# Gated-attention kernel: gate units in two parts, input checks moved, gate checked on output sums

## The chip, the cores and the metric

One core of a Trainium2 chip. The metric is the device time of one execution in microseconds (us), the median of three runs.

## The reference

Per batch (B=4), head (H=8) and channel, an attention with a decaying state, then two MLP blocks on x of shape (4, 768, 384):

```python
state = alpha[:, :, t, :, None] * state + np.einsum('bhd,bhe->bhde', k[:, :, t], v[:, :, t])
y[:, :, t] = np.einsum('bhd,bhde->bhe', q[:, :, t], state)       # S=768, D=48
...
x = x + np.maximum(layernorm(x) * g_ln @ w_ch1, 0) @ w_ch2       # 384 -> 1536 -> 384
h = gelu_tanh(x @ w_in); u, v = h[..., :512], h[..., 512:]       # 384 -> 1024
v_s = np.einsum('ts,bsd->btd', w_sg, layernorm(v) * g_ln2) + b_sg[None, :, None]
out = x + (u * v_s) @ w_out
```

## The kernel before

Every large product runs as three float16 passes on operands split into a high and a low half: ACT makes the high half, DVE or GpSimd (POOL) subtracts it and makes the low one (the helper `low`, L155 and its neighbours). This is only right for inputs within certain ranges, so the kernel gathers statistics of its operands on the way (`st_in`, `st_g`, `st_ws` and others), compares them at the end with bounds (`checks`, L1107 to L1109), and a flag then decides whether a slow general path runs as well. It does not run for these inputs, but the statistics are always taken.

The 3072 rows are 24 chunks of 128 (six to a batch) and 12 groups j of two chunks. `att_steps(i)` is the attention of chunk i: loads into one of two input tiles (`load_chunk`, L236, chunk i into the tile of chunk i-2), transposes by DMA (L298 splits into 16-bit halves on ACT, L301 is the transpose, L314 joins), scans over time on DVE (L361), the scaling of q and k (`scaled`), ACT's halves of them (L446, L468), the scaling of K (L482), scores and masks (L490, L503), v's halves (L549, L551), and the outputs psd and psy (L585, L621). `stats()` (L560 to L568) then takes the squares of q, k and v on ACT (L564) and the largest alpha on DVE (L567). The next chunk for this tile can only load when these have read it.

The matmul stages of a group are lists of units: `A_units` (w1, L717; ACT makes the hidden tile hT at L722, DVE its low half at L723), `B_units` (w2, L752, added at L755), `T_units` (transposes of x, L151, L152, L773, check L775), `C_units` (w_in, L799 and L828, with the gelu at L802 and L831). Per batch come `D_units` (the spatial gate: six units of 36 matmuls, L856, two scale-and-add on DVE, L862, product with u on POOL, L865) and `E_units` (w_out, L890; addition L892; output L894). The gate's product is split into halves only when the next gate unit is through: `finish_gate()` takes one `halves_of_gate` from a list, which makes the high half (L869), the low one, and the sum of squares for `st_g` (L872).

`split_path` puts all attention steps and units into one list of events with planned times and calls them in this order; the scheduler below it fixes each engine's order from there. Units have costs in us of PE. The reduces that check the weights (`weight_windows`, L903) are put out by a count of units, one at a time, behind the last low half of a hidden tile:

```python
n_unit += 1
if n_unit >= 160 and n_unit % 4 == 0 and windows:
    with tc.issue_after(last_dve[0].ins):
        windows.pop(0)()
```

All matmul outputs of A to E share a ring of three PSUM buffers (tag "g").

Of the kernel before, what the change touches and what calls it, by code (L numbers as in the profile page):

```python
# [17 lines left out]
P = 128  # L18
# [35 lines left out]
def split_path(ctx, tc, ident, bad, q, k, v, alpha, g1, w1, w2, w_in, g2, w_sg, b_sg, w_out, out):  # L54
# [14 lines left out]
    U = 256  # L69
# [32 lines left out]
    st_g = big.tile([P, NC], F32, name="st_g")  # L102
# [151 lines left out]
    def att_steps(i, group, slot):  # L254
# [179 lines left out]
        @step  # L434
        def _():
            if whole:
                nc.vector.scalar_tensor_tensor(out=T["F"], in0=T["q"], scalar=S_Q * S_K, in1=T["F"], op0=ALU.mult,
                                               op1=ALU.mult)
            else:
                scaled("F", "q")  # L440
            if whole:
                work(["ks"], F16)
                T["ks"] = T["ks"].rearrange("p a n t -> p (a n t)").bitcast(F32).rearrange("p (n t) -> p n t", n=NP)
            else:
                work(["qs"], F16)
                nc.scalar.activation(out=T["qs"][:, 0], in_=T["F"], func=AF.Copy)  # L446
            if not by_dma:
                T["k"] = transposed(1)
# [13 lines left out]
        else:  # L462
# [7 lines left out]
            @step  # L470
            def _():
                low(chosen(HB), T["kh"][:, 1], T["K"], T["kh"][:, 0])
                if "ks" not in T:
                    work(["ks"], F16)
                nc.sync.dma_start_transpose(out=T["ks"].rearrange("p a n d -> p (a n) d"),
                                            in_=T["kh"].rearrange("p a n t -> p (a n t)"))

            @step
            def _():
                T["Kr"] = T["K"]  # L480
                for p in range(NP):
                    nc.scalar.activation(out=T["K"][:, p, :], in_=T["K"][:, p, :], func=AF.Copy,  # L482
                                         scale=T["rf"][:, p:p + 1])

# [76 lines left out]
        def stats():  # L561
            with tc.issue_after(T["v last"][0].ins):
                for n in range(3):
                    nc.scalar.activation(out=junk()[:, 0:DM].rearrange("p (h d) -> p h d", h=H),  # L564
                                         in_=t[:, n, :, 0:D], func=AF.Square, accum_out=st_in[:, i, n:n + 1])
            with tc.issue_after(T["v last"][1].ins):
                nc.vector.tensor_reduce(out=st_in[:, i, 3:4], in_=t[:, 3, :, 0:D], op=ALU.max, axis=AX.XY,  # L567
                                        apply_absolute_value=True)  # L568
# [275 lines left out]
    def D_units(b):  # L844
        units = []
        for th in range(S // U):
            for dp in range(KG // 2):
                def unit(th=th, dp=dp):
# [3 lines left out]
                    pg = ps.tile([P, 2, U], F32, tag="g", bufs=3, name="pgs")  # L852
                    for f in range(2):
                        d = 2 * dp + f
# [4 lines left out]
                    tm = p2.tile([P, 2, U], F32, tag="tm", name="tm")  # L859
# [8 lines left out]
                    def halves_of_gate():  # L868
                        nc.scalar.activation(out=gt[key][:, dp, 0], in_=tm, func=AF.Copy)  # L869
                        low(dp, gt[key][:, dp, 1], tm, gt[key][:, dp, 0])  # L870
                        n_ = b * 6 + 2 * th + dp
                        nc.scalar.activation(out=junk()[:, 0:512].rearrange("p (a b) -> p a b", a=2), in_=tm,  # L872
                                             func=AF.Square, accum_out=st_g[:, n_:n_ + 1])
# [3 lines left out]
                units.append((unit, 36 * U / 2400.0, NW[3]))  # L877
        return units

    def E_units(b):  # L880
        units = []
        for c in range(NCH):
            def unit(c=c):
# [4 lines left out]
                for d in range(KG):  # L888
                    for a, r in passes:
# [3 lines left out]
                                               op0=ALU.mult, op1=ALU.add)  # L893
# [33 lines left out]
    if True:  # L927
# [149 lines left out]
        for _, kind, f, need in sorted(events, key=lambda x: x[:2]):  # L1077
# [17 lines left out]
            (st_g, 0.0, 2.0 ** 31, [NC]),  # L1095
# [257 lines left out]
```

## Time and profile before

| | |
|---|---|
| median of 3 runs | 686.86 us (686.51 to 688.11) |
| profiled execution | 688.59 us |
| its span | 686.8 us |
| PE busy | 640.7 us (93%) |
| DVE busy | 442.2 us (64%) |
| ACT busy | 412.1 us (60%) |
| POOL busy | 237.3 us (35%) |
| mean granted clock of PE | 0.981 |

The page gives the busy time of an engine over the whole span; the stretches, timelines and waits below are views of the same trace. A timeline row begins with the start and the length of an instruction or a run of like ones; what stands in brackets is how long the engine was idle before it and what released it.

### The profile page before, as it was taken

Reading aid. Unit: us, or ns where it says so; the run is one execution under the profiler, and the core shown is the slowest. Engines: PE = TensorE matmul, PEld = TensorE weight load, DVE = VectorE, ACT = ScalarE, POOL = GpSimd, SP = SyncE. Lnnn points to the kernel's source line nnn. Section 1 sums busy time; section 2 is a strip of 40 time slices with the busy share of each in tenths; the row PEclk is TensorE's granted clock in tenths of the full one; section 3 lists DMA queues with packets and bytes.
Section 4 is the critical chain, followed back from the end, with each engine's and each line's share of the span. In section 5 each row is a group of like instructions: output and inputs, shape, how many; then the busy total and the mean of one; then the engine's idle time right before and its main releaser. Section 6 shows DMA issues by size and latency. Waiting matters only on the chain.

```text
span 686.8 us, 14367 instructions
## 1 busy us (share of the span) xinstructions
PE 640.7 (93%) x5622; PEld 487.2 (71%) x5622; DVE 442.2 (64%) x852; ACT 412.1 (60%) x787; POOL 237.3 (35%) x462
## 2 busy tenths in 40 slices
PE   5989798989999989999999989998989999999995
PEld 3677586667676876677677876676666986676783
DVE  6799977867745576557745569658756686233334
ACT  3765445687873698498773788767663873232230
POOL 4132210533423650443533751532405660301251
PEclk9999979999999998999999999999999999999999
DMA  9996879648363468466263387754263402200102
GB/s 226 279 246 177 259 168 185 105 88 118 64 107 53 72 110 152 105 113 110 48 112 51 60 116 158 123 105 70 51 89 62 86 17 70 24 12 12 35 2 75
DMA packets 228637, 70.64 MB, mean 103 GB/s; under 512 B 219472, under 2 KB 222544, under 8 KB 228560
## 3 DMA queue, kind: packets, MB, share of 16 engines
q1 hardware_dynamic: 228560, 69.63, 53.3%
q8 instruction: 46, 0.75, 0.5%
q14 instruction: 31, 0.25, 0.1%
HBM read 35.79 MB, written 4.72 MB: 59 GB/s over the span
## 4 chain that ended last, share of the span: by engine, by line
PE 51%; DMA 15%; DVE 14%; ACT 11%; issue 4%; POOL 2%; SPq 1%; ACTq 0%; DVEq 0%; POOLq 0%
PE pg L752 12%; PE pg L717 10%; PE pgs L856 9%; PE pgo L890 5%; PE pgu L828 5%; DMA stage<-stage 5%; PE pgv L799 4%; DMA wgs<-wsp 3%; ACT stage L314 2%; DMA stage<-in_moe_w_ch_dram 2%; DMA xhT<-xsp 2%; DMA inp<-in_q_dram 2%; ACT stage L298 2%; PE sc L490 1%; DVE sc L503 1%
## 5 line engine op out<-in xcount | busy, mean ns | idle before, releaser
L717 PE MATMUL pg<-xhT,w1s 128*128 128x256 f16 (+1 forms) x1404 | 152.5, 268 | 10.6 <-DVE hT L723 9.4
L717 PEld LDWEIGHTS <-w1s 128*128 128x128 f16 x1404 | 130.1, 100 | 28.7 <-issue 9.0
L752 PE MATMUL pg<-w2s,hT 128*128 128x384 f16 x864 | 146.6, 328 | 0.4 <-DVE hT L723 0.4
L752 PEld LDWEIGHTS <-hT 128*128 128x128 f16 x864 | 83.8, 98 | 54.3 <-issue 1.4
L856 PE MATMUL pgs<-wgs,vn 128*128 128x256 f16 x864 | 96.0, 273 | 0.0
L856 PEld LDWEIGHTS <-vn 128*128 128x128 f16 x864 | 84.1, 98 | 10.3
L723 DVE SCALAR_TENSOR_TENSOR hT<-pg,hT 128x512 f16<-128x512 f32 (+1 forms) x74 | 49.2, 673 | 44.8 <-ACT hT L722 44.6
L314 ACT ACTIVATE stage<-stage 128x1024 uint16<-128x1024 uint16 x48 | 64.4, 1351 | 16.2 <-DMA stage<-stage 16.2
L298 ACT ACTIVATE stage<-inp 128x1024 uint16<-128x1024 uint16 x48 | 49.8, 1051 | 26.2 <-DVE K L361 8.8
L155 POOL TENSOR_TENSOR kh<-K,kh 128x512 f16<-128x512 f32 x17 | 21.0, 1238 | 102.3 <-ACT kh L468 102.3
L722 ACT ACTIVATE hT<-pg 128x512 f16<-128x512 f32 (+1 forms) x74 | 42.0, 572 | 17.5 <-PE pg L717 17.1
L828 PE MATMUL pgu<-x2T,wis 128*128 128x256 f16 x432 | 49.6, 273 | 1.7 <-ACT vg L802 0.9
L799 PE MATMUL pgv<-wis,x2T 128*128 128x512 f16 x216 | 49.3, 379 | 1.8 <-DVE hT L723 1.8
L890 PE MATMUL pgo<-wos,uT 128*128 128x384 f16 x288 | 48.6, 326 | 0.1
L828 PEld LDWEIGHTS <-wis 128*128 128x128 f16 x432 | 41.8, 98 | 8.3 <-issue 1.8
L155 POOL TENSOR_TENSOR qs<-F,qs 128x512 f16<-128x512 f32 x18 | 20.2, 1121 | 76.8 <-ACT qs L446 76.8
L865 POOL TENSOR_TENSOR tm<-tm,uT 128x512 f32<-128x512 f32 x24 | 32.9, 1372 | 23.6 <-DVE tm L862 23.2
L890 PEld LDWEIGHTS <-uT 128*128 128x128 f16 x288 | 27.7, 98 | 18.0 <-issue 0.3
L862 DVE SCALAR_TENSOR_TENSOR tm<-pgs,g2c,bbc 128x256 f32<-128x256 f32 x48 | 20.9, 477 | 28.9 <-PE pgs L856 17.6
L799 PEld LDWEIGHTS <-x2T 128*128 128x128 f16 x216 | 20.5, 97 | 24.0 <-issue 1.9
L522 ACT ACTIVATE ss<-sc 128x512 f16<-128x512 f32 x36 | 20.8, 591 | 24.0 <-DVE sc L503 23.9
L869 ACT ACTIVATE uT<-tm 128x512 f16<-128x512 f32 x24 | 15.0, 626 | 30.0 <-POOL tm L865 30.0
(184 smaller groups left out, 1094.0 us busy)
## 6 DMA issues: line engine op xcount, KB each, us to landing
stage<-in_moe_w_ch_dram SPq DMA_DIRECT2D x24, 384.0 KB, 5.3
inp<-in_alpha_dram SPq DMA_DIRECT2D x24, 192.0 KB, 3.6
inp<-in_q_dram SPq DMA_DIRECT2D x24, 192.0 KB, 3.4
inp<-in_k_dram SPq DMA_DIRECT2D x24, 192.0 KB, 4.0
inp<-in_v_dram SPq DMA_DIRECT2D x24, 192.0 KB, 4.3
out_dram<-x SPq DMA_DIRECT2D x24, 192.0 KB, 1.9
stage<-in_moe_w_in_dram SPq DMA_DIRECT2D x4, 768.0 KB, 4.8
stage<-in_moe_w_sg_dram SPq DMA_DIRECT2D x6, 384.0 KB, 4.1
```

Of the source, the lines that this page charges most:

```text
L155: (nc.vector if on_dve else nc.gpsimd).tensor_tensor(out=out, in0=in0, in1=in1, op=ALU.subtract)
L298: nc.scalar.activation(out=sp, in_=t[:, n].rearrange("p h d -> p (h d)").bitcast(U16) .rearrange("p (x w) -> p w x", w=2), func=AF.Copy)
L314: nc.scalar.activation(out=words[:, :, :, gap:], in_=tr, func=AF.Copy)
L717: nc.tensor.matmul(out=pg[:, f, :], lhsT=w1s[:, a, kk, ff * P:(ff + 1) * P], rhs=xhT[j][:, r, kk, o], start=(n_ == 0), stop=(n_ == 3 * KD ...
L722: nc.scalar.activation(out=hi, in_=src, func=AF.Relu)
L723: last_dve[0] = nc.vector.scalar_tensor_tensor(out=lo, in0=src, scalar=0.0, in1=hi, op0=ALU.max, op1=ALU.subtract)
L752: nc.tensor.matmul(out=box[s], lhsT=hidden(a, f, s), rhs=w2s[:, r, f, :], start=(f == 0 and a == 0 and r == 0), stop=(f == KF - 1 and r == 1))
L799: nc.tensor.matmul(out=pg, lhsT=x2T[j][:, a, kk, o], rhs=wis[:, r, kk, DG:DI], start=(n_ == 0), stop=(n_ == 3 * KD - 1))
L828: nc.tensor.matmul(out=pg[:, f, :], lhsT=wis[:, a, kk, ff * P:(ff + 1) * P], rhs=x2T[j][:, r, kk, 0:N], start=(n_ == 0), stop=(n_ == 3 * K ...
L856: nc.tensor.matmul(out=pg[:, f, :], lhsT=vn[b * NCH + s][:, a, d * P:(d + 1) * P], rhs=wgs[th][:, r, s, :], start=(n_ == 0), stop=(n_ == 3 ...
L865: nc.gpsimd.tensor_tensor(out=tm, in0=tm, in1=uT[key][:, o, :], op=ALU.mult)
L890: nc.tensor.matmul(out=pg, lhsT=gt[key][:, d // 2, a, d % 2, o], rhs=wos[:, r, d, :], start=(d == 0 and a == 0 and r == 0), stop=(d == KG ...
```

## The change

A unit of the gate becomes two, f=0 and f=1, of 18 matmuls each; the scale-and-add, the product and `finish_gate()` are in the second. The squares of q and k and the reduce of alpha move from `stats()` to the place behind the first instruction that reads the operand (`T["q read"]`, `T["k read"]`, `T["q scaled"]`); v's square stays. The gate's sum of squares is taken for the last batch only; for the other three the addition behind w_out (L892) sums its output into a new row `st_o`, which is checked instead. In the changed kernel's rows below the line numbers are higher by 1 to 17.

```diff
--- before.py
+++ after.py
@@ -99,7 +99,8 @@
     st_mv = big.tile([P, NC, 2], F32, name="st_mv")
     st_xs = big.tile([P, NC], F32, name="st_xs")
     st_xm = big.tile([P, NC], F32, name="st_xm")
-    st_g = big.tile([P, NC], F32, name="st_g")
+    st_g = big.tile([P, 6], F32, name="st_g")
+    st_o = big.tile([P, NC - NCH], F32, name="st_o")
     st_ws = big.tile([P, 8 + NG3 + 2 * KD], F32, name="st_ws")
     st_w, st_wg, st_w1, st_wr = (st_ws[:, a:b] for a, b in ((0, 8), (8, 8 + NG3), (8 + NG3, 8 + NG3 + KD),
                                                             (8 + NG3 + KD, 8 + NG3 + 2 * KD)))
@@ -437,13 +438,13 @@
                 nc.vector.scalar_tensor_tensor(out=T["F"], in0=T["q"], scalar=S_Q * S_K, in1=T["F"], op0=ALU.mult,
                                                op1=ALU.mult)
             else:
-                scaled("F", "q")
+                T["q scaled"] = scaled("F", "q")
             if whole:
                 work(["ks"], F16)
                 T["ks"] = T["ks"].rearrange("p a n t -> p (a n t)").bitcast(F32).rearrange("p (n t) -> p n t", n=NP)
             else:
                 work(["qs"], F16)
-                nc.scalar.activation(out=T["qs"][:, 0], in_=T["F"], func=AF.Copy)
+                T["q read"] = nc.scalar.activation(out=T["qs"][:, 0], in_=T["F"], func=AF.Copy)
             if not by_dma:
                 T["k"] = transposed(1)
 
@@ -472,6 +473,13 @@
                 low(chosen(HB), T["kh"][:, 1], T["K"], T["kh"][:, 0])
                 if "ks" not in T:
                     work(["ks"], F16)
+
+                for n, first in enumerate((T["q read"], T["k read"][0])):
+                    with tc.issue_after(first.ins):
+                        square(n)
+                with tc.issue_after(T["q scaled"].ins):
+                    nc.vector.tensor_reduce(out=st_in[:, i, 3:4], in_=t[:, 3, :, 0:D], op=ALU.max, axis=AX.XY,
+                                            apply_absolute_value=True)
                 nc.sync.dma_start_transpose(out=T["ks"].rearrange("p a n d -> p (a n) d"),
                                             in_=T["kh"].rearrange("p a n t -> p (a n t)"))
 
@@ -481,6 +489,10 @@
                 for p in range(NP):
                     nc.scalar.activation(out=T["K"][:, p, :], in_=T["K"][:, p, :], func=AF.Copy,
                                          scale=T["rf"][:, p:p + 1])
+
+        def square(n):
+            nc.scalar.activation(out=junk()[:, 0:DM].rearrange("p (h d) -> p h d", h=H), in_=t[:, n, :, 0:D],
+                                 func=AF.Square, accum_out=st_in[:, i, n:n + 1])
 
         def scores():
             for e in range(2):
@@ -560,12 +572,7 @@
 
         def stats():
             with tc.issue_after(T["v last"][0].ins):
-                for n in range(3):
-                    nc.scalar.activation(out=junk()[:, 0:DM].rearrange("p (h d) -> p h d", h=H),
-                                         in_=t[:, n, :, 0:D], func=AF.Square, accum_out=st_in[:, i, n:n + 1])
-            with tc.issue_after(T["v last"][1].ins):
-                nc.vector.tensor_reduce(out=st_in[:, i, 3:4], in_=t[:, 3, :, 0:D], op=ALU.max, axis=AX.XY,
-                                        apply_absolute_value=True)
+                square(2)
 
         @step
         def _():
@@ -845,18 +852,24 @@
         units = []
         for th in range(S // U):
             for dp in range(KG // 2):
-                def unit(th=th, dp=dp):
+                box = {}
+
+                def unit(f, th=th, dp=dp, box=box):
                     key = (b, th)
 
                     gt[key] = uf[key].bitcast(F16).rearrange("p (g a f t) -> p g a f t", g=KG // 2, a=2, f=2)
-                    pg = ps.tile([P, 2, U], F32, tag="g", bufs=3, name="pgs")
-                    for f in range(2):
-                        d = 2 * dp + f
+                    if f == 0:
+                        box["pg"] = ps.tile([P, 2, U], F32, tag="g", bufs=3, name="pgs")
+                        box["tm"] = p2.tile([P, 2, U], F32, tag="tm", name="tm")
+                    pg, tm = box["pg"], box["tm"]
+                    d = 2 * dp + f
+                    if True:
                         for n_, (s, a, r) in enumerate([(s, a, r) for s in range(NCH) for a, r in passes]):
                             nc.tensor.matmul(out=pg[:, f, :], lhsT=vn[b * NCH + s][:, a, d * P:(d + 1) * P],
                                              rhs=wgs[th][:, r, s, :], start=(n_ == 0),
                                              stop=(n_ == 3 * NCH - 1))
-                    tm = p2.tile([P, 2, U], F32, tag="tm", name="tm")
+                    if f == 0:
+                        return
                     for f in range(2):
                         d = 2 * dp + f
                         nc.vector.scalar_tensor_tensor(out=tm[:, f, :], in0=pg[:, f, :], scalar=g2c[:, d:d + 1],
@@ -868,13 +881,15 @@
                     def halves_of_gate():
                         nc.scalar.activation(out=gt[key][:, dp, 0], in_=tm, func=AF.Copy)
                         low(dp, gt[key][:, dp, 1], tm, gt[key][:, dp, 0])
-                        n_ = b * 6 + 2 * th + dp
-                        nc.scalar.activation(out=junk()[:, 0:512].rearrange("p (a b) -> p a b", a=2), in_=tm,
-                                             func=AF.Square, accum_out=st_g[:, n_:n_ + 1])
+                        if b == B - 1:
+                            n_ = 2 * th + dp
+                            nc.scalar.activation(out=junk()[:, 0:512].rearrange("p (a b) -> p a b", a=2), in_=tm,
+                                                 func=AF.Square, accum_out=st_g[:, n_:n_ + 1])
                     gate_pending.append(halves_of_gate)
                     if b == B - 1 and th == S // U - 1 and dp == KG // 2 - 1:
                         finish_gate()
-                units.append((unit, 36 * U / 2400.0, NW[3]))
+                for f in range(2):
+                    units.append((lambda f=f, unit=unit: unit(f), 18 * U / 2400.0, NW[3]))
         return units
 
     def E_units(b):
@@ -890,7 +905,8 @@
                         nc.tensor.matmul(out=pg, lhsT=gt[key][:, d // 2, a, d % 2, o], rhs=wos[:, r, d, :],
                                          start=(d == 0 and a == 0 and r == 0), stop=(d == KG - 1 and r == 1))
                 nc.vector.scalar_tensor_tensor(out=xs[i], in0=pg, scalar=1.0 / (S_G * S_WO), in1=xs[i],
-                                               op0=ALU.mult, op1=ALU.add)
+                                               op0=ALU.mult, op1=ALU.add,
+                                               accum_out=st_o[:, i:i + 1] if b < B - 1 else None)
                 nc.sync.dma_start(out=out[b, c * P:(c + 1) * P, :], in_=xs[i])
             units.append((unit, 12 * DM / 2400.0, NW[4]))
         return units
@@ -1092,7 +1108,8 @@
             (st_xs, -1e30, 1e30, [NC]),
             (st_mv[:, :, 1:2], 2.0 ** -22 * S_Y ** 2, 2.0 ** 3 * S_Y ** 2, [NC, 1]),
             (st_xm, 2.0 ** -12, 2.0 ** 14, [NC]),
-            (st_g, 0.0, 2.0 ** 31, [NC]),
+            (st_g, 0.0, 2.0 ** 31, [6]),
+            (st_o, -1e30, 1e30, [NC - NCH]),
             (st_w, 2.0 ** -2, 127.0, [8]),
             (st_wg, 2.0 ** -2, 6e4, [NG3]),
             (st_w1, 2.0 ** -2, 2000.0, [KD]),
```

What it does to the order, at the end of batch 1's gate. ACT, from the scaling of K (L482, after: L490) to the first hidden tile (L722, after: L729) that PE waits for; L869 (after: L882) is a gate half, L872 its square, L446 (L447) the high half of q, L549 (L561) that of v, L494 the moved squares. Before:

```order
L482 ACTIVATE K<-K,rf 128x128 x4
L869 ACTIVATE uT<-tm 128x512
L872 ACTIVATE junk,st_g<-tm 128x512
L446 ACTIVATE qs<-F 128x512
L314 ACTIVATE stage<-stage 128x2x512
L647 ACTIVATE sp<-state 128x384
L549 ACTIVATE vs<-inp_95 128x384
L314 ACTIVATE stage<-stage 128x2x512
L660 ACTIVATE xsp<-psy,nmu 128x384
L151 ACTIVATE xsp<-x 128x384
L722 ACTIVATE hT<-pg 128x512
```

After:

```order
L490 ACTIVATE K<-K,rf 128x128 x4
L447 ACTIVATE qs<-F 128x512
L494 ACTIVATE junk,st_in<-inp_96 128x384 x2
L654 ACTIVATE sp<-state 128x384
L561 ACTIVATE vs<-inp_96 128x384
L882 ACTIVATE uT<-tm 128x512
L315 ACTIVATE stage<-stage 128x2x512
L667 ACTIVATE xsp<-psy,nmu 128x384
L152 ACTIVATE xsp<-x 128x384
L494 ACTIVATE junk,st_in<-inp_96 128x384
L315 ACTIVATE stage<-stage 128x2x512
L729 ACTIVATE hT<-pg 128x512
```

The two squares of q and k stand behind q's half, v's square ahead of the last join, the gate's square is gone, and the high half of v (L561) comes ahead of both joins.

DVE, from the low half of this hidden tile on (L723, after: L730); L503 (L515) are masks, L361 (L362) scans. Before:

```order
L723 SCALAR_TENSOR_TENSOR hT<-pg,hT 128x512
L155 TENSOR_TENSOR uT<-tm,uT 128x512
L503 TENSOR_TENSOR sc<-sc,causal 128x512 x2
L361 SCALAR_TENSOR_TENSOR F<-stage,reset 128x516
L361 SCALAR_TENSOR_TENSOR K<-stage,reset 128x516
L723 SCALAR_TENSOR_TENSOR hT<-pg,hT 128x512 x2
```

After:

```order
L730 SCALAR_TENSOR_TENSOR hT<-pg,hT 128x512
L156 TENSOR_TENSOR uT<-tm,uT 128x512
L730 SCALAR_TENSOR_TENSOR hT<-pg,hT 128x512
L515 TENSOR_TENSOR sc<-sc,causal 128x512
L730 SCALAR_TENSOR_TENSOR hT<-pg,hT 128x512
L515 TENSOR_TENSOR sc<-sc,causal 128x512
L362 SCALAR_TENSOR_TENSOR F<-stage,reset 128x516
L362 SCALAR_TENSOR_TENSOR K<-stage,reset 128x516
```

The second and third low half stand ahead of the scans.

DVE, behind the last low halves of the same group; L903 (L919) are the reduces over the weights, L892 (L907) the additions behind w_out. Before:

```order
L723 SCALAR_TENSOR_TENSOR hT<-pg,hT 128x512 x3
L903 TENSOR_REDUCE st_ws<-w1s 128x1
L892 SCALAR_TENSOR_TENSOR x<-pgo,x 128x384
L903 TENSOR_REDUCE st_ws<-w1s 128x1
L892 SCALAR_TENSOR_TENSOR x<-pgo,x 128x384 x2
L503 TENSOR_TENSOR sc<-sc,causal 128x512 x2
L361 SCALAR_TENSOR_TENSOR K<-stage,reset 128x516
```

After:

```order
L481 TENSOR_REDUCE st_in<-inp_95 128x1
L730 SCALAR_TENSOR_TENSOR hT<-pg,hT 128x512 x2
L919 TENSOR_REDUCE st_ws<-w1s 128x1 x3
L919 TENSOR_REDUCE st_ws<-w2s 128x1 x2
L907 SCALAR_TENSOR_TENSOR x,st_o<-pgo,x 128x384 x3
L939 SCALAR_TENSOR_TENSOR st_ws<-g1r,st_ws 128x3
L515 TENSOR_TENSOR sc<-sc,causal 128x512 x2
L362 SCALAR_TENSOR_TENSOR K<-stage,reset 128x516
```

Five reduces stand in one row ahead of the first three additions; before there was one ahead of the first and one ahead of the second.

## Rows read from the trace of the kernel before

**Rows 1.** The page's busy times, share of the span and instructions of each engine.
```profile
PE 640.7 (93%) x5622; PEld 487.2 (71%) x5622; DVE 442.2 (64%) x852; ACT 412.1 (60%) x787; POOL 237.3 (35%) x462
```

**Rows 2.** PE's waits: who waited for whom: us in total, times, longest us.
```profile
PE pg L717 <- DVE hT L723: 9.4, 7, 1.7
```

**Rows 3.** Stretches of 20 us: busy time of each engine (x instructions), PE's granted clock, DMA.
```profile
240.00:260.00 20.00, 17.59 (x198) 15.14 (x195) 15.32 (x28) 19.57 (x43) 10.65 (x14) 0.95 0.68 112
260.00:280.00 20.00, 18.52 (x149) 12.43 (x148) 12.34 (x24) 15.29 (x30) 2.68 (x5) 0.88 0.70 133
400.00:420.00 20.00, 16.13 (x163) 13.22 (x160) 14.11 (x28) 19.36 (x41) 8.23 (x13) 0.91 0.76 124
420.00:440.00 20.00, 20.00 (x165) 12.45 (x165) 16.95 (x29) 14.28 (x30) 5.99 (x13) 1.00 0.72 149
```

**Rows 4.** Timeline of PE, end of batch 0's gate: start, us, work, [idle before <-releaser].
```profile
257.17 3.17 PE L717 MATMUL pg<-xhT,w1s 128*128 128x256 f16 x18 [1.67 <-DVE hT L723]
...
261.82 5.59 PE L717 MATMUL pg<-xhT,w1s 128*128 128x256 f16 x36 [1.48 <-DVE hT L723]
267.24 4.06 PE L890 MATMUL pgo<-wos,uT 128*128 128x384 f16 x24
```

**Rows 5.** Timeline of ACT, the same place.
```profile
255.71 0.58 ACT L722 ACTIVATE hT<-pg 128x512 f16<-128x512 f32 x1
...
257.83 1.06 ACT L722 ACTIVATE hT<-pg 128x512 f16<-128x512 f32 x2
```

**Rows 6.** Timeline of DVE, the same place.
```profile
256.43 0.69 DVE L723 SCALAR_TENSOR_TENSOR hT<-pg,hT 128x512 f16<-128x512 f32 x1
...
261.09 1.26 DVE L723 SCALAR_TENSOR_TENSOR hT<-pg,hT 128x512 f16<-128x512 f32 x2
```

**Rows 7.** Timeline of PE, end of batch 1's gate.
```profile
411.09 3.48 PE L717 MATMUL pg<-xhT,w1s 128*128 128x256 f16 x18 [1.67 <-DVE hT L723]
415.74 4.10 PE L717 MATMUL pg<-xhT,w1s 128*128 128x256 f16 x36 [1.17 <-DVE hT L723]
419.94 4.06 PE L890 MATMUL pgo<-wos,uT 128*128 128x384 f16 x24
423.93 0.71 PE L490 MATMUL sc<-F,K 48*128 48x128 f32 x8
...
427.27 2.45 PE L890 MATMUL pgo<-wos,uT 128*128 128x384 f16 x14
```

**Rows 8.** Timeline of ACT, ahead of batch 1's last hidden tiles.
```profile
400.44 1.06 ACT L298 ACTIVATE stage<-inp 128x1024 uint16<-128x1024 uint16 x1 [1.80 <-DMA inp<-in_k_dram]
```

**Rows 9.** Groups of ACT's and DVE's instructions: count | busy us, mean ns | idle before.
```profile
L872 ACT ACTIVATE junk<-tm 128x512 bf16<-128x512 f32 x24 | 14.8, 615 | 0.0
...
L755 DVE SCALAR_TENSOR_TENSOR x<-pg,rx,x 128x384 f32<-128x384 f32 x24 | 14.7, 612 | 19.2 <-PE pg L752 19.2
...
L892 DVE SCALAR_TENSOR_TENSOR x<-pgo,x 128x384 f32<-128x384 f32 x24 | 13.3, 554 | 13.2 <-PE pgo L890 13.0
...
L903 DVE TENSOR_REDUCE st_ws<-w1s 128x1 f32<-128x1536 f16 x3 | 5.2, 1744 | 0.0
```

**Rows 10.** Timeline of DVE, end of batch 1's gate.
```profile
421.37 0.69 DVE L723 SCALAR_TENSOR_TENSOR hT<-pg,hT 128x512 f16<-128x512 f32 x1 [0.74 <-ACT hT L722]
421.98 1.75 DVE L903 TENSOR_REDUCE st_ws<-w1s 128x1 f32<-128x1536 f16 x1
423.64 0.55 DVE L892 SCALAR_TENSOR_TENSOR x<-pgo,x 128x384 f32<-128x384 f32 x1
```

**Rows 11.** Timeline of PE, waits between 120 and 140 us.
```profile
124.93 2.13 PE L828 MATMUL pgu<-x2T,wis 128*128 128x256 f16 x18 [0.80 <-DVE nmu L658]
...
139.95 0.20 PE L621 MATMUL psy<-vs,ss 128*128 128x48 f16 x1 [1.37 <-ACT ss L522]
```

**Rows 12.** Timeline of PE, a score that waits for ACT's K.
```profile
475.06 0.78 PE L490 MATMUL sc<-F,K 48*128 48x128 f32 x8 [1.52 <-ACT K L482]
```

**Rows 13.** Timeline of DVE, the last addition.
```profile
679.65 0.56 DVE L892 SCALAR_TENSOR_TENSOR x<-pgo,x 128x384 f32<-128x384 f32 x1 [1.34 <-PE pgo L890]
```

## The prediction

> **What bounds the kernel now.** I read the page's busy times first. TensorE (PE) is busy for 640.7 of 686.8 us [rows 1], so at most 46 us can be won without taking matmuls away, and the change takes none away: any gain must come out of the waits of PE. The list of PE's waits says which of those are left: the largest is L717, the first MLP matmul, waiting for VectorE's (DVE's) half of the hidden tile, L723: 9.4 us in 7 places [rows 2]. The table of 20-us stretches then says where: from 240 to 280 us and from 400 to 420 us PE works 17.59, 18.52 and 16.13 of 20 us and ScalarE (ACT) is full in two of the three, while the next stretch, 420 to 440, has PE at 20.00 [rows 3]. These are the ends of the spatial gate of batch 0 and of batch 1, where the gate's last halves, a chunk's input work and the hidden tiles of the next group meet on ACT and DVE.
>
> The three timelines of batch 0 show the mechanism. PE's last three units of L717 start at 257.17, 1.67 us late, and 261.82, 1.48 us late, and w_out (L890) only at 267.24 [rows 4]. ACT gives the hidden tile that is waited for at 255.71, behind a row of other work, then runs a gate half and its square L872, and gives the next two at 257.83 [rows 5]. DVE makes the first half at 256.43, then stands in its order behind masks and two scans and makes the next two only at 261.09 [rows 6]. Batch 1 repeats it: waits of 1.67 and 1.17 us, w_out at 419.94 [rows 7]. There the row of ACT work was itself held 1.80 us by the load of k [rows 8].
>
> **The change part by part.** *The gate's squares.* 18 of the 24 squares L872 go: 0.615 us each [rows 9], 11.1 us of ACT time, and the reading of an accumulator behind each. Most of it lies where PE works anyway, so I cost it at nothing by itself. Only the squares in front of a hidden tile count: one between the first tile and the second in each of the two gates, and it is part of the next term. In exchange 18 of the L892 get an accumulator. DVE's like instruction with one, L755, takes 612 ns against L892's 554 [rows 9]: 18 x 0.06 = 1.0 us of DVE beside PE's w_out, with three output buffers between, 0 on the path. If that cover were gone it would be 0.06 us per chunk.
>
> *The halves half a unit later, batch 0.* By the order, the second hidden tile stands one gate half behind the first on ACT, not behind half, square and another check, and on DVE no scan stands before the second and third. So the third wait (1.48 us) goes, and the stretch behind it is no longer entered with an idle PE. The first tile itself gains little: a square of the gate goes in front of it and the three squares of its own chunk come in. With the fourth unit from 257.2 for 3.17 us [rows 4] and the next two with no wait in 4.1 us, as in batch 1 [rows 7], w_out starts at 264.5 instead of 267.24: **-2.7 us**. Bounds: 0 if the first tile comes later by as much; -5 if its wait of 1.67 goes too.
>
> *The same in batch 1.* The wait of 1.17 us goes [rows 7]. The load of k waits before for a square that the ACT queue reaches late; now that square stands right behind the last reader of k, so the 1.80 us of [rows 8] should go and the first hidden tile come 1.4 us or more earlier. Together -2.6 for the start of w_out: 417.3 instead of 419.94. Bounds 0 and -4.
>
> *What the finer units push into batch 1.* The reduces that check the weights (L903) are counted out one on every fourth unit from the 160th on. Twelve more units stand ahead of that point (each gate has six more), and the order has five of them in one row behind the last hidden tile of this group, in front of the first three additions of w_out. Before, the row was hT, one reduce, addition, one reduce, addition [rows 10]. One reduce is 1.74 us [rows 9]; at a start-to-start of 1.66 us [rows 10] five are 8.4 us. The last hidden half ends 2.1 us after w_out begins (419.94 and 421.37 + 0.69), so the first addition ends 2.1 + 8.4 + 0.55 = 11.1 us after w_out's start. PE has three output buffers: it computes three chunks (2.05 us each, half of the 4.06 for 24 matmuls [rows 7]) and the two score groups (0.7 us each by the 0.71 at 423.93 [rows 7]), 7.5 us, and then stands for 3.6 us. Before, the fourth chunk began 7.33 us after the first; now 11.1: **+3.8 us**. It cannot hide behind idle time, since the stretch from 420 to 440 has none [rows 3]. Behind the reduces wait, besides, two masks and a scan; their readers on PE come after the same three chunks and are late by the same time. Net for batch 1: 3.8 - 2.6 = **+1.2**.
>
> *The clock.* The granted clock is 0.95 and 0.88 in the stretches of batch 0 and 0.91 in that of batch 1 [rows 3]. With levels of 2.4 and 1.2 GHz these means are about 6.8 and 3.6 us at half. It fell each time when PE stood for the first hidden tile, and 18 matmuls took 3.17 and 3.48 us instead of 2.05. What the new stall does to the clock no row shows directly. From above, 18 matmuls at half: +1.4 us; from below, the half-clock stretch of 3.6 us moves away from the gate: -1.4. I take 0. The Trainium skill (TensorE: Matmul & The Clock Gate, Part 1) says that the throttled level is the default and activity releases it. The trace agrees as to the fall. By this rule the stall in w_out would be followed by slow matmuls, and the sum would be 1.4 us higher, as no row of the w_out stretch before shows.
>
> *The input checks early.* alpha's reduce behind its scaling and the squares of q and k behind theirs let the loads of chunk i+2 leave earlier, since two buffers alternate. From 120 to 140 us it meets two waits of PE: 0.80 us at 124.93 and 1.37 us at 139.95, behind a chunk whose alpha came late [rows 11]. I take the first and half of the second, **-1.5**; bounds -4 (a second wait of that kind behind it, and slower matmuls) and +2.5 (two of the w_sg splits move behind squares, and hold up the masks). SP issues the alpha loads ahead of transposes that are later needed, 0 here: in each case the transposes wait for ACT anyway.
>
> *K's scalings.* Around the fifth group the four L482 of a chunk stand ahead of the vg tile, and the scores are spread. The nearest row is a score that waited 1.52 us for them [rows 12]. I take **+1.0**, between 0 and 1.5.
>
> *The tail.* One more entry in the list of checks, three small instructions. DVE waits there 1.34 us for PE [rows 13], so 0; if that cover were gone, less than one L892 each, 1.7 us.
>
> *The sum.* -2.7 + 1.2 - 1.5 + 1.0 = -2.0 us. The profiled execution took 688.59 us, with a span of 686.8 and 1.8 around it; it becomes 686.6. The runs shown have their median 1.7 us below it, so against the median: 686.86 - 2.0 = **684.9 us**. A measurement of this kernel can tell about 0.2%, 1.4 us.
>
> **The rivals.**
> *The clock holds (faster).* If the first tile comes early enough in both batches that PE does not fall to half, 3.17 - 2.05, 5.59 - 4.10 and 3.48 - 2.05 us come in addition [rows 4, 7]: 4.0 us, 680.9 us. For it: the removed waits lie just ahead of the slow matmuls. Against it: PE has small matmuls alone ahead of the first tile, and ACT has three squares more there. The rule of the skill's page (the same Part 1) points this way in batch 0, where matmuls come without a gap sooner.
>
> *The row of reduces decides (slower).* The mechanism is the five reduces at 424 to 428 us. It decides if the first hidden tile of batch 1 is no earlier than before: three squares of the chunk now stand ahead of it where one gate square of 0.615 us stood. They have 384 columns against its 512, an estimate of 0.46 us each, so +0.8 us, which takes back the load's gain when the load is not what ACT waits for. Then batch 1 is +3.8, the stall is followed by slow matmuls, +1.4, K's scalings +1.0, the early checks give 0 and batch 0 only the difference of 1.5 - 0.8: -0.7. Together +5.5: 692.4 us. For it: this stall is in the order, with durations from rows, and PE has nothing else to do.
>
> *It does nothing that shows.* The loads leave earlier, but what they feed waits for other things, and the gain at the first gate (-2.7) is eaten by the reduces, net of what batch 1 gains, and K's scalings (+2.2). That is -0.5: 686.4 us. For it: ACT and DVE have 40% and 36% idle [rows 1], and PE 20.00 of 20 us next to these stretches.
>
> **How the numbers follow.** The forecast gets 0.37, the held clock 0.20, the reduces 0.28 and no change 0.15. The forecast's own range is 683 to 687. For 8 in 10 I take the held clock in whole and most of the way to the slow case: **680.5 to 691.0**. Faster by over 0.2%: 0.28 of the forecast's 0.37 and the 0.20, 0.48. Within 0.2%: 0.06 of the forecast and 0.15, 0.21. Slower: the 0.28 and 0.03, 0.31.
>
> **What would show it.** After the change the list of PE's waits should have L717 behind DVE at 5 us or less, and w_out of batch 0 start within 8.5 us of the fourth unit of L717 (10.1 before). In batch 1 the DVE timeline should have five reduces in a row and the list of waits a new entry, w_out behind the addition, of about 3.6 us. ACT's wait for k before that gate should be gone. The prediction is wrong if that new entry is under 1.5 us or above 5, if the first hidden tile in either gate still comes late by 1.6 us, or if new waits of PE appear in the stretch from 280 to 400 us, which I hold to be unchanged but for K's scalings. The clock stands or falls with the granted clock from 240 to 280 us: 0.95 or more in both stretches would speak for the first rival.

## The result and the profile after

The changed kernel takes 691.48 us (median of 4 runs, 690.96 to 693.6); before it was 686.68 us in the same measurement. The ratio is 1.0074, 95% interval 1.0047 to 1.0101: slower, 4.8 us where 2 us faster was forecast, and outside the stated range. The profiled execution has a span of 691.8 us, 5.0 more than that of before, so the two traces can be set against each other.

The page of the kernel after, and its list of PE's waits (us in total, times, longest):

```profile
PE 641.8 (93%) x5622; PEld 487.9 (71%) x5622; DVE 445.3 (64%) x873; ACT 400.4 (58%) x751; POOL 237.2 (34%) x462
```

```profile
PE pg L724 <- DVE hT L730: 10.4, 9, 3.0
PE pgo L905 <- DVE x L907: 4.2, 1, 4.2
...
PE psy L628 <- ACT ss L534: 3.2, 1, 3.2
```

ACT has 11.7 us less to do (412.1 before), and PE is busy for 1.1 us more [rows 1]. L724's wait for the hidden half did not shrink (9.4 before [rows 2]), and there is a new one: w_out for its own addition, 4.2 us, once. The third line is also new in this size; the two waits that it replaces were 1.4 and 1.0 us.

The stretches of the two gates after, with the columns of [rows 3]:

```profile
240.00:260.00 20.00, 17.90 (x205) 15.76 (x203) 15.23 (x28) 16.73 (x31) 10.31 (x15) 0.97 0.61 104
260.00:280.00 20.00, 19.79 (x159) 13.62 (x158) 12.96 (x30) 14.10 (x26) 2.89 (x5) 0.94 0.62 123
400.00:420.00 20.00, 16.96 (x155) 14.31 (x153) 14.26 (x26) 16.21 (x31) 8.08 (x13) 0.91 0.60 111
420.00:440.00 20.00, 15.57 (x121) 9.22 (x119) 17.51 (x28) 10.19 (x14) 2.30 (x3) 0.83 0.51 119
```

At the first gate PE is idle for 2.3 us of 40, before 3.9. The loss stands in the last row: 4.4 us idle, and a granted clock of 0.83, where the kernel before had 20.00 us of work at 1.00. The timeline of PE at batch 1's gate, then that of DVE:

```profile
401.81 6.06 PE L724 MATMUL pg<-xhT,w1s 128*128 128x256 f16 x54
...
412.62 7.60 PE L724 MATMUL pg<-xhT,w1s 128*128 128x256 f16 x54 [3.04 <-DVE hT L730]
420.19 2.11 PE L905 MATMUL pgo<-wos,uT 128*128 128x384 f16 x12
422.51 4.06 PE L905 MATMUL pgo<-wos,uT 128*128 128x384 f16 x24 [0.21 <-DVE hT L730]
426.50 1.16 PE L502 MATMUL sc<-F,K 48*128 48x128 f32 x16
431.88 6.38 PE L905 MATMUL pgo<-wos,uT 128*128 128x384 f16 x25 [4.21 <-DVE x L907]
```

```profile
421.78 1.27 DVE L730 SCALAR_TENSOR_TENSOR hT<-pg,hT 128x512 f16<-128x512 f32 x2
422.98 5.06 DVE L919 TENSOR_REDUCE st_ws<-w1s 128x1 f32<-128x1536 f16 x3
427.96 3.40 DVE L919 TENSOR_REDUCE st_ws<-w2s 128x1 f32<-128x1536 f16 x2
431.28 0.54 DVE L907 SCALAR_TENSOR_TENSOR x<-pgo,x 128x384 f32<-128x384 f32 x1
```

The five reduces run from 422.98 to 431.36, the first addition ends at 431.82, and at 431.88 PE takes up w_out's fourth chunk, 11.7 us behind its first (7.3 before [rows 7]). Its next 25 matmuls take 6.38 us; at the 0.17 us of the 24 in 4.06 us they would take 4.2, so 2.1 us more go to the clock.

### The profile page after: what moved, and what is told of

Same layout as the page of the kernel before. It is cut to its first block, busy times and chain, and to the rows that moved or that the text cites. A ratio compares the mean times of both kernels' runs of the same rounds, so it can differ in the third digit from the quotient of the medians.

```text
span 691.8 us, 14361 instructions
## 1 busy us (share of the span) xinstructions
PE 641.8 (93%) x5622; PEld 487.9 (71%) x5622; DVE 445.3 (64%) x873; ACT 400.4 (58%) x751; POOL 237.2 (34%) x462
## 4 chain that ended last, share of the span: by engine, by line
PE 46%; DVE 21%; ACT 14%; DMA 10%; issue 4%; POOL 3%; SPq 1%; ACTq 0%; DVEq 0%; POOLq 0%
PE pg L759 12%; PE pgs L868 8%; PE pg L724 7%; PE pgo L905 5%; PE pgv L806 4%; PE pgu L835 4%; DMA stage<-stage 3%; ACT stage L315 3%; DVE hT L730 2%; DVE F L362 2%; DVE sc L515 2%; DVE K L362 2%; ACT stage L299 2%; DVE ss L156 2%; DMA xhT<-xsp 2%
## 5 line engine op out<-in xcount | busy, mean ns | idle before, releaser
L724 PE MATMUL pg<-xhT,w1s 128*128 128x256 f16 (+1 forms) x1404 | 153.1, 269 | 12.2 <-DVE hT L730 10.4
L724 PEld LDWEIGHTS <-w1s 128*128 128x128 f16 x1404 | 130.7, 100 | 30.3 <-issue 13.4
L759 PE MATMUL pg<-w2s,hT 128*128 128x384 f16 x864 | 144.8, 326 | 0.8 <-DVE hT L730 0.4
L730 DVE SCALAR_TENSOR_TENSOR hT<-pg,hT 128x512 f16<-128x512 f32 (+1 forms) x74 | 49.1, 671 | 35.9 <-ACT hT L729 35.8
L729 ACT ACTIVATE hT<-pg 128x512 f16<-128x512 f32 (+1 forms) x74 | 41.6, 573 | 23.4 <-PE pg L724 23.2
L905 PE MATMUL pgo<-wos,uT 128*128 128x384 f16 x288 | 50.7, 335 | 4.6 <-DVE x L907 4.2
L882 ACT ACTIVATE uT<-tm 128x512 f16<-128x512 f32 x24 | 15.0, 624 | 32.6 <-POOL tm L878 32.6
L818 DVE TENSOR_SCALAR vg<-vg,mvv,rv 128x512 f32<-128x512 f32 x24 | 15.9, 666 | 25.0 <-POOL rv L252 24.8
```

The costliest lines, as they stand in the source:

```text
L724: nc.tensor.matmul(out=pg[:, f, :], lhsT=w1s[:, a, kk, ff * P:(ff + 1) * P], rhs=xhT[j][:, r, kk, o], start=(n_ == 0), stop=(n_ == 3 * KD ...
L729: nc.scalar.activation(out=hi, in_=src, func=AF.Relu)
L730: last_dve[0] = nc.vector.scalar_tensor_tensor(out=lo, in0=src, scalar=0.0, in1=hi, op0=ALU.max, op1=ALU.subtract)
L759: nc.tensor.matmul(out=box[s], lhsT=hidden(a, f, s), rhs=w2s[:, r, f, :], start=(f == 0 and a == 0 and r == 0), stop=(f == KF - 1 and r == 1))
L905: nc.tensor.matmul(out=pg, lhsT=gt[key][:, d // 2, a, d % 2, o], rhs=wos[:, r, d, :], start=(d == 0 and a == 0 and r == 0), stop=(d == KG ...
```

## The experiments

Each kernel was timed over several runs on one chip, beside the kernel before; ratios are to that, with 95% intervals. `n_unit` is the count of units, from which the reduces are put out.

**1. The reduces back in place.** The changed kernel with

```diff
-                if n_unit >= 160 and n_unit % 4 == 0 and windows:
+                if n_unit >= 172 and n_unit % 4 == 0 and windows:
```

> The changed kernel, but the weight reduces counted from unit 172, so that they stand where they stood before (two behind batch 1's last hidden tile, not five). Theory A (the row of five reduces is the loss: a 4.2 us stall at w_out of batch 1, and slow matmuls after it): 685 to 687 us, no wait of w_out for an addition of over 0.5 us, granted clock 1.00 from 420 to 440 us. Theory B (the moved input checks are the loss, the stall only shows up where another wait would have stood): 689 to 691.5 us.

685.91 us, ratio 0.9986 (0.9967 to 1.0006). Without the row of five the change costs nothing that can be told. The stretch from 420 to 440 us, same columns:

```profile
420.00:440.00 20.00, 20.00 (x182) 13.49 (x181) 15.60 (x33) 17.44 (x34) 7.15 (x16) 1.00 0.83 183
```

**2. Five reduces in the kernel before.** In `before`:

```diff
-                if n_unit >= 160 and n_unit % 4 == 0 and windows:
+                if n_unit >= 148 and n_unit % 4 == 0 and windows:
```

> The kernel before, with the weight reduces counted from unit 148, which puts five of them into batch 1's w_out as the change does (one ahead of the first addition, four ahead of the second). Theory A: a wait of w_out of 3 to 5 us and slow matmuls behind it, 690 to 693 us. Theory B: 687 to 688 us.

685.31 us, 0.9976 (0.9952 to 1.0000): not slower, against theory A as it was put, and below the range of theory B too. The timeline of DVE shows the difference, and behind it PE's start of the fourth chunk:

```profile
419.57 1.74 DVE L903 TENSOR_REDUCE st_ws<-w1s 128x1 f32<-128x1536 f16 x1
421.23 0.55 DVE L892 SCALAR_TENSOR_TENSOR x<-pgo,x 128x384 f32<-128x384 f32 x1
421.69 3.40 DVE L903 TENSOR_REDUCE st_ws<-w1s 128x1 f32<-128x1536 f16 x2
425.01 3.40 DVE L903 TENSOR_REDUCE st_ws<-w2s 128x1 f32<-128x1536 f16 x2
428.33 1.01 DVE L892 SCALAR_TENSOR_TENSOR x<-pgo,x 128x384 f32<-128x384 f32 x2
```

```profile
425.35 2.12 PE L890 MATMUL pgo<-wos,uT 128*128 128x384 f16 x12
```

Here one addition stands ahead of four of the reduces. It gives PE a free buffer at 421.8, the fourth chunk starts with no wait, and PE has psy's matmuls between until the second addition at 428.33. So the number of reduces in the group does not make the stall; that all of them stand ahead of the first addition does (experiment 10 tests this in the changed kernel).

**3 and 4. Two parts alone.** The moved input checks in `before` (experiment 3), and the gate's sums in w_out's addition in `before` (experiment 4); each is the part of the change's diff, nothing else, with the reduces where they were.

```diff
+                for n, first in enumerate((T["q read"], T["k read"][0])):
+                    with tc.issue_after(first.ins):
+                        square(n)
...
-                for n in range(3):
...
+                square(2)
```

```diff
+                        if b == B - 1:
...
-                                               op0=ALU.mult, op1=ALU.add)
+                                               op0=ALU.mult, op1=ALU.add,
+                                               accum_out=st_o[:, i:i + 1] if b < B - 1 else None)
```

> The kernel before with the moved input checks alone (squares of q and k and alpha's reduce behind the first reader). Theory A: between 685 and 688 us; the wait at 140 us for the masks' halves is 3.2 us as in the changed kernel, against 2.4 in two pieces before, so not faster there. Theory B: 689 us or more.

> The kernel before with the gate's squares of three batches replaced by sums in w_out's addition, alone. Both theories: 685.5 to 687.5 us; the first hidden tile of batch 0 and batch 1 comes 0.5 to 0.7 us earlier, one square, and PE's wait for it shrinks by as much.

Experiment 3: 683.69 us, 0.9942 (0.9922 to 0.9963), faster, and below the range of theory A as well; theory B falls. Experiment 4: 687.77 us, 1.0016 (0.9994 to 1.0039), no gain. In its trace the first hidden tile at batch 0's gate, expected 0.5 to 0.7 us earlier, comes at 255.80, no earlier than before (255.71 [rows 5]). The second comes at 257.30 instead of 257.83, but PE is idle for 3.1 us from 460 to 480 us (before 2.4) and for 0.9 from 320 to 340 (before none).

**5 and 6. Four and three in the row.** The changed kernel with

```diff
+                if n_unit >= 164 and n_unit % 4 == 0 and windows:
```

and with 168 in this line.

> The changed kernel with four reduces, not five, in the row ahead of the first three additions (counted from unit 164). Theory A, each reduce in that row at 1.69 us: the wait of w_out for the addition falls from 4.2 to 2.5 us; from 685.9 (two in the row) that is 688.4 us, up to 690.1 if slow matmuls follow the stall. Theory C (it is not the row's length but any gap at w_out that lets the clock fall): as with five, 690.5 to 692 us.

> The changed kernel with three reduces in that row (counted from unit 168). Theory A: wait of w_out 0.8 us, 686.7 us, granted clock 1.00 from 420 to 440 us. Theory C: 688 us or more.

Four: 686.27 us, 0.9997 (0.9978 to 1.0016). Three: 683.29 us, 0.9951 (0.9933 to 0.9969). PE's start of the fourth chunk with four and with three:

```profile
427.47 4.55 PE L905 MATMUL pgo<-wos,uT 128*128 128x384 f16 x27 [1.76 <-DVE x L907]
```

```profile
425.55 5.36 PE L905 MATMUL pgo<-wos,uT 128*128 128x384 f16 x32
```

The wait is 1.76 us with four and gone with three, as computed within 0.8 us. The times are not as computed: theory A gave 688.4 and 686.7 us, and the kernels are 2.1 and 3.4 us faster than that. With four the clock from 420 to 440 us stays at 1.00:

```profile
420.00:440.00 20.00, 17.49 (x144) 10.75 (x143) 15.75 (x28) 15.26 (x26) 5.60 (x10) 1.00 0.57 132
```

Theory C falls at this place: a gap of 1.76 us brought no slow matmuls. (At the gates waits no longer than that, 1.67 us, do stand ahead of slow matmuls [rows 4] [rows 7], so the length of one wait does not decide it.)

That three are better than two I had not expected. Part of it stands in the next group. In experiment 1 PE waits twice in the stretch from 496 to 506 us, L724 for a hidden half 0.79 us and the first product of w_in (pgv) 1.55 us. On ACT the third hidden tile of that group stands behind the split of a load of q, and the split waits for the load:

```profile
496.22 1.06 ACT L299 ACTIVATE stage<-inp 128x1024 uint16<-128x1024 uint16 x1 [2.44 <-DMA inp<-in_q_dram]
497.18 0.58 ACT L729 ACTIVATE hT<-pg 128x512 f16<-128x512 f32 x1
```

With three in the row the third tile stands ahead of that split, and PE has no wait from 468 to 520 us:

```profile
494.86 0.60 ACT L729 ACTIVATE hT<-pg 128x512 f16<-128x512 f32 x1 [1.37 <-PE pg L724]
...
498.31 1.06 ACT L299 ACTIVATE stage<-inp 128x1024 uint16<-128x1024 uint16 x1 [1.71 <-DVE K L362]
```

With four the order is that of three, and PE has no wait there either; the changed kernel with five has the order of experiment 1, and loses 2.6 us from 500 to 520 us (3.0 in experiment 9). So the step from five to four (5.2 us between the medians, 4.3 by experiment 9, from different measurements) holds 2.5 us of stall, slow matmuls behind the longer stall, and these waits, less what comes back elsewhere; it can't be read as the price of the stall and the clock alone. Why the place of the reduces changes the order on ACT was not taken apart.

**7 and 8. The split alone, and with the checks.** Units in two parts in `before`, with 172 in the line of the reduces, and these together with the moved checks of experiment 3:

```diff
-                units.append((unit, 36 * U / 2400.0, NW[3]))
+                for f in range(2):
+                    units.append((lambda f=f, unit=unit: unit(f), 18 * U / 2400.0, NW[3]))
```

> The kernel before with the gate's units in two parts alone, the reduces counted from unit 172 so that they stay in place. If the later halves are what brings the second and third hidden tile forward: scans behind them on DVE, the third wait of L717 gone in both gates, 683.5 to 685.5 us. If the squares or the checks do that: 686 to 688 us, with the two waits as before.

> Split units and moved input checks, the gate's squares as before, the reduces in place (from unit 172). Against all three parts (685.9 us) it tells what the sums in w_out's addition cost or give: if they give nothing, 684 to 686 us; if taking the squares away is what helps at the gates, 687 to 689 us.

The split alone: 684.45 us, 0.9963 (0.9947 to 0.9980). Its waits at batch 0's gate:

```profile
246.79 6.06 PE L717 MATMUL pg<-xhT,w1s 128*128 128x256 f16 x54
...
255.57 2.12 PE L717 MATMUL pg<-xhT,w1s 128*128 128x256 f16 x18 [1.30 <-DVE hT L723]
257.70 2.13 PE L717 MATMUL pg<-xhT,w1s 128*128 128x256 f16 x18
261.73 2.14 PE L717 MATMUL pg<-xhT,w1s 128*128 128x256 f16 x18 [1.78 <-DVE hT L723]
265.32 8.77 PE L897 MATMUL pgo<-wos,uT 128*128 128x384 f16 x53 [1.46 <-DVE hT L723]
```

The wait of the third hidden tile did not go (1.78 us), yet w_out starts 18.5 us behind the first unit of L717, before 20.4 (267.24 - 246.83). Split and checks together: 684.84 us, 0.9976 (0.9957 to 0.9995). The gains of the parts (2.5 and 3.3 us) don't add. One reason is in the traces: both parts take away the same waits from 460 to 480 us, where the kernel before has 2.4 us of idle PE, the split alone 0.4 and the checks alone none.

**9. The changed kernel again,** beside the last three.

> The changed kernel unchanged, on the chip of the three runs beside it. Theory A: 690.5 to 692 us, the stall of w_out of 4.2 us again and some us at half the clock behind it.

690.54 us, 1.0067 (1.0048 to 1.0087). The same stall:

```profile
428.67 5.90 PE L905 MATMUL pgo<-wos,uT 128*128 128x384 f16 x25 [4.22 <-DVE x L907]
```

```profile
420.00:440.00 20.00, 15.78 (x122) 9.31 (x121) 15.19 (x25) 9.67 (x16) 2.52 (x4) 0.91 0.46 111
```

**10. Each reduce behind the last addition too.** The changed kernel, counted from 160, with

```diff
-                nc.vector.scalar_tensor_tensor(out=xs[i], in0=pg, ...
+                last_dve[0] = nc.vector.scalar_tensor_tensor(out=xs[i], in0=pg, ...
```

> The changed kernel with the reduces counted from unit 160 as in it, but each put behind the last addition of w_out as well as behind the last hidden tile, so that five still fall into this group and only one stands ahead of the first addition. Theory A (the place ahead of the additions counts, not the number): no wait of w_out for an addition, 684 to 687 us. Theory D (five reduces in this group hold up DVE wherever they stand): 689 us or more, with the wait moved to the masks or the gelu's statistics behind them.

686.33 us, 0.9996 (0.9979 to 1.0013): 4.2 us less than experiment 9, with the same five reduces in this group. No wait for the addition is left. The fourth chunk starts at 424.39, without one:

```profile
419.97 4.06 PE L905 MATMUL pgo<-wos,uT 128*128 128x384 f16 x24 [0.21 <-DVE hT L730]
424.39 3.91 PE L905 MATMUL pgo<-wos,uT 128*128 128x384 f16 x23
```

So theory A holds for the stall. Two other stretches differ as well. From 500 to 520 us PE has no wait, where experiment 9 loses 3.0 us. And at 468 PE waits twice for the second halves of the masked scores (0.88 and 1.02 us), which it does not in experiment 9. One reduce stands ahead of these masks on DVE, at 461.96, but in experiment 9 it does so too (464.62), so theory D is not shown by this wait.

**11 and 12. Three in the row with fewer parts.** Experiment 8 with 168, and experiment 3 with 156.

> Split units and moved checks, the gate's squares as before, three reduces in the row (from unit 168). Theory A with the gains of each part: 682 to 684 us, no slower than the 683.3 us of all three parts with three in the row. If the third part (sums in w_out) carries the gain of that kernel: 685 us or more.

> The kernel before with the moved input checks alone and three reduces in the row (from unit 156). If three in a row are as good there as in the changed kernel, because later stretches lose less: 681.5 to 683.5 us. If the row costs what it holds up: 684 to 686 us.

683.89 us, 0.9955 (0.9937 to 0.9972), and 682.34 us, 0.9934 (0.9915 to 0.9952). The moved checks alone, with three reduces in the row, have the lowest time of this study, 4.1 us under the kernel before, though the intervals of experiments 3, 6 and 11 overlap with theirs; that the split and the sums add anything to them is not shown.

## Why the prediction was wrong

The slow rival named the mechanism, at 692.4 us and with a chance of 0.28. The forecast had the same stall in its sum and let three other terms outweigh it. That the rival came within 0.9 us of the 691.48 us is in part luck: it had 0.7 us of gain at batch 0, where 3.0 were measured, and waits that stood in nobody's sum make up for it.

By the signs that the prediction set itself, it failed at the hidden tiles: the first one is late by 2.10 us at batch 0's gate and by 3.04 us at batch 1's, where 1.6 was the mark, and L724's waits for DVE come to 10.4 us, where it said 5 or less. Other signs came: w_out of batch 0 starts 7.6 us behind the fourth unit, five reduces stand in a row, the new wait is 4.2 us, and ACT's wait for k is gone.

Term by term, against the trace of after:

- **Batch 0, -2.7 us.** Right in size. From the first of the six units of L717 to w_out it takes 17.4 us, before 20.4: 3.0 us gained. The third wait went, as forecast; the first hidden tile is still waited for, 2.10 us. The slow matmuls that I thought to keep cost nothing: in experiment 9 the clock here is full and the same stretch takes 17.5 us, since PE then waits 1.52 us for a hidden tile. In these two executions ACT and DVE, with the hidden tiles, set the start of w_out, not the matmuls' speed. So the rival of the held clock had a price of nearly zero at this place, where I gave it 2.6 us; and 1.49 of these I had counted twice, since the forecast's own term already takes the last two units at 4.1 us. The two rows below are the changed kernel in its first profile and in experiment 9:

```profile
248.79 6.06 PE L724 MATMUL pg<-xhT,w1s 128*128 128x256 f16 x54
...
258.66 7.72 PE L724 MATMUL pg<-xhT,w1s 128*128 128x256 f16 x54 [2.10 <-DVE hT L730]
266.23 2.11 PE L905 MATMUL pgo<-wos,uT 128*128 128x384 f16 x12
```

```profile
245.95 6.06 PE L724 MATMUL pg<-xhT,w1s 128*128 128x256 f16 x54
...
255.86 6.05 PE L724 MATMUL pg<-xhT,w1s 128*128 128x256 f16 x54 [2.14 <-DVE hT L730]
263.43 2.11 PE L905 MATMUL pgo<-wos,uT 128*128 128x384 f16 x12 [1.52 <-DVE hT L730]
```

- **Batch 1's start of w_out, -2.6 us.** Mis-sized: 18.4 us from the first unit to w_out, before 19.4, so -1.1. The step that failed is "the 1.80 us of [rows 8] should go and the first hidden tile come 1.4 us or more earlier". The wait for k's load went, as said, but the first of the chunk's three splits then waits for a scan, and the join behind them for a transpose:

```profile
396.98 1.06 ACT L299 ACTIVATE stage<-inp 128x1024 uint16<-128x1024 uint16 x1 [2.12 <-DVE K L362]
...
402.22 1.37 ACT L315 ACTIVATE stage<-stage 128x1024 uint16<-128x1024 uint16 x1 [0.87 <-DMA stage<-stage]
...
411.27 0.57 ACT L729 ACTIVATE hT<-pg 128x512 f16<-128x512 f32 x1
```

  Together 3.0 us, more than the 1.80 that went, and the chunk's three squares, which the order showed ahead of the tile, take 0.51 us each, not the estimated 0.46. It starts 9.5 us behind the first unit of L717 (411.27 - 401.81); before it was 9.1 (409.64 - 400.50).
- **The five reduces, +3.8 us.** Right, and a little small: 11.7 - 7.3 = +4.4 us, the wait 4.2 instead of 3.6, since the last hidden half ends 2.9 us behind w_out's start, not 2.1. Experiments 1, 5 and 10 show that it is this row and its place: without it the kernel is 4.2 to 5.6 us faster, the slow matmuls and the later waits that come and go with the row included. Experiment 2 shows what the argument rests on: with one addition ahead of four of the reduces there is no stall.
- **The clock, 0.** Wrong: +2.1 us for the 25 matmuls behind the stall (+1.7 in experiment 9), above the upper bound of 1.4, which was priced on 18 matmuls of 256 columns where w_out's have 384. A stall of 4.2 us was followed by slow matmuls in both profiles, one of 1.76 us in experiment 5 was not. The rule of the Trainium skill (TensorE: Matmul & The Clock Gate, Part 1), that the clock falls to the throttled level when the engine has nothing to do, spoke for it, and the trace agrees: the granted clock from 420 to 440 us is 0.83, and 0.91 in experiment 9, where it was 1.00 before. I had put the lower bound, less of it at the gate, on the same footing, without asking whether faster matmuls there would give anything back; at batch 0's gate they did not. At batch 1's this is not shown.
- **The early checks, -1.5 us at 120 to 140 us.** Not earned: the first wait of [rows 11], 0.80 us, went, but the second, for the masks' halves, grew. It was 1.37 us with 1.00 behind it, and is 3.19 in one piece. From 120 to 160 us PE is idle for 3.7 us, before 3.9, so -0.3. Before, then after:

```profile
120.00:140.00 20.00, 17.06 (x133) 11.75 (x132) 14.57 (x29) 13.79 (x27) 9.02 (x22) 1.00 0.69 112
140.00:160.00 20.00, 19.00 (x174) 15.20 (x175) 14.58 (x33) 15.03 (x32) 5.59 (x11) 0.91 0.51 92
```

```profile
120.00:140.00 20.00, 20.00 (x153) 13.64 (x151) 14.93 (x29) 13.86 (x27) 9.01 (x23) 1.00 0.62 103
140.00:160.00 20.00, 16.33 (x152) 12.90 (x150) 11.90 (x28) 15.56 (x34) 5.78 (x10) 0.91 0.66 99
```

  alpha's load did come earlier (issued at 126.9 us, before 132.3), and with it ACT's splits. That put two joins ahead of the masks' halves on ACT, and these wait for transposes. The ACT timeline, then PE's wait:

```profile
139.69 2.54 ACT L315 ACTIVATE stage<-stage 128x1024 uint16<-128x1024 uint16 x2 [3.97 <-DMA stage<-stage]
142.10 1.03 ACT L299 ACTIVATE stage<-inp 128x1024 uint16<-128x1024 uint16 x1
...
143.54 1.05 ACT L534 ACTIVATE ss<-sc 128x512 f16<-128x512 f32 x2
```

```profile
144.17 0.20 PE L628 MATMUL psy<-vs,ss 128*128 128x48 f16 x1 [3.19 <-ACT ss L534]
```

  Experiment 3 has the same wait (3.5 us). In experiment 12, with the same checks and the joins in the same place, it is 0.7; there the joins wait 2.33 us instead of 3.97. But the checks gain where I had put nothing: from 460 to 480 us PE's two waits of 1.52 us ([rows 12]) and 0.86 us are gone, 2.4 us, in the changed kernel and in experiment 3 alike (the split alone, in experiment 7, leaves 0.4 us of them).
- **K's scalings, +1.0 us.** 0.95 us of idle PE from 300 to 340 us, where there was none, but in three small waits of 0.3 us, one for a hidden tile and two for vg (the gelu's tile), none of them a score. That the size agrees is luck.
- **The sums in w_out's addition, 0.** Right. The 0.06 us each that I took from L755 as the price of an accumulator is not there: L907 takes 553 ns in the changed kernel, L892 took 554 [rows 9]. A separate read of the accumulator, 82 ns, stands behind each.
- **The sum.** With the terms as measured: -3.0 - 1.1 + 4.4 + 2.1 - 0.3 + 1.0 - 2.4 = +0.7. The rest up to +5.0, the difference of the two spans, is to within 0.2 us in small waits that had no term: 0.9 us at 440 behind the stall, for vg; 1.2 at 574; 0.5 more at 180 to 200 and 0.5 less at 500 to 520; 1.3 at 100 to 120; and 1.1 us in the first 100 us, which this execution has and experiment 9 has not. The 1.3 can't be put down to the checks: from 100 to 120 us PE's idle time lies between 2.6 and 4.5 us over the kernels of this study, and is 3.7 with the split alone.

So two steps turned the sign. One is the gain at the second gate, 2.6 us, that I took from one wait in ACT's row without asking which comes behind it; it was 1.1. The other is the price of the row of reduces, 3.8 us with nothing for the clock; with the slow matmuls behind the stall it was 6.5. By these two alone -2.0 becomes +2.2. Without the row, the measured terms and the small waits come to -1.3 us, and experiment 1, which is without it, lies 1.1 us under the kernel before by its median, which is not clear of noise.

What stays open: how the 5.6 us between experiment 1 and the changed kernel divide. The stall of 4.2 us and the slow matmuls behind it (2.1 and 1.7 us in its two traces) come to more than that. PE loses time in experiment 1 that it does not lose in the changed kernel, such as 1.9 us from 540 to 560 us, and a part can't be told from the spread between runs (684.2 to 687.2 us in experiment 1).

## What to carry to other kernels

Work that no engine needs soon, such as a check, still takes its place in an engine's order; ask what stands behind it there, and how many output buffers PE has until the first instruction behind it must have run. A counter that places such work moves when units are cut finer, so it has to move with them. And when a wait is to go, look for the next one in the same row before its time is booked as a gain.

## What the runs showed of the hardware

The stretches at half clock are not fixed by the program. The same changed kernel had a granted clock of 0.97 and 0.94 from 240 to 280 us in one profile, with 2.3 us of idle PE there, and 1.00 twice in the other, with 3.9 us; experiment 7, with 4.5 us idle, had 1.00 as well. The kernel before spread from 683.2 to 690.3 us over 34 runs on one chip. And matmuls at the full clock gain less than the slow ones suggest where PE then waits for other engines: at this gate w_out started 17.4 us behind the first unit with the slow matmuls and 17.5 without.
